# Spectral kernel on one core: the mixed signal stored by groups of eight positions, result tiles taken from two or three groups, wider mode matmuls

## The chip, the core and the metric

One Trainium2 chip, one of its cores. A time is the device time of one execution in microseconds (us). The kernel before: 379.84 us, the median of three runs (379.36 to 381.79). Engines: PE multiplies matrices (its weight loads are listed as PEld), VectorE is DVE, ScalarE is ACT, GpSimd is POOL; SP only issues DMAs here, and POOL issues some.

## The reference

Two layers on x of 8 batches, S = 5696 positions, D = 128 channels. The first convolves every channel with a filter h of the same length; the second mixes 64 Fourier modes, adds the result to its input, and adds a ReLU of a channel product:

```python
L = 2 * S
y = irfft(rfft(x, n=L, axis=1) * rfft(h, n=L, axis=0)[None], n=L, axis=1)[:, :S]
X = rfft(y, axis=1)[:, :64]
Yr = einsum('bmd,mde->bme', X.real, w_r) - einsum('bmd,mde->bme', X.imag, w_i)
Yi = einsum('bmd,mde->bme', X.real, w_i) + einsum('bmd,mde->bme', X.imag, w_r)
u = y + irfft(Yr + 1j * Yi, n=S, axis=1)      # 64 modes, the others zero
out = u + maximum(u @ w_ch, 0)                # float32, 8 x 5696 x 128
```

## The kernel before

A position s is written s = 64 q + p, with q from 0 to 88 and p from 0 to 63. The convolution is done as a transform over q and one over p, with 90 frequencies k. Batches go in four **pairs** `g_` of two (`b` = 0, 1).

*Up to about 255 us*, pair after pair: the transform of x (`a_tile`), the second transform (`second`), the product with the filter (`products`), and the way back over p. The result Z goes to DRAM (`zscr`), and the 64 modes of each pair are summed beside it in one PSUM bank. At the end of a pair two copies with a factor, `XT`, take these modes to SBUF (lines 757 to 760): one of 256 columns on ScalarE, and one of 128 on ScalarE, for the last pair on VectorE. `XT` holds, for each batch, 64 columns of the negated imaginary part, then the real, then the imaginary part.

*The mix* (`mix`, line 828) is 128 matmuls, two for each mode, whose weights are the mode's matrix and whose moving operand are 16 columns of `XT` (two parts of eight batches, gathered from a step of 192 columns). Between its parts PE makes the Z part of the first three u tiles (`u_z` with `alone`). Then the copies Y, eight transposes, and the copies C.

*The last stage* makes u and the result. A **u tile** (`u_tile`, line 809) is one batch, eight values of p and all 89 values of q: 16 matmuls with 89 columns on Z (`ZT`, `S4a`, `S4b`) and two with 356 columns for the modes (`IBs`, `C`), in two of the eight PSUM banks. One copy takes its 712 columns to `UT`, a row of 5696 positions per batch, in natural order: position 64 q + p in column 64 q + p, so that runs of eight columns are written. The copies go to ScalarE and VectorE five to three, and in the last pair to ScalarE alone. A **chunk** of 16 values of p (two u tiles for each batch) is loaded from `zscr` by two DMAs; there are five buffers (`NC`), and chunk i + 5 is asked for once chunk i is used up (`load_zt`).

A **result tile** (`o_tile`, line 863) is four matmuls with 256 columns: the weights are 128 positions of `UT`, 44 columns apart, and the moving operand `WI` holds `w_ch` beside a unit matrix. ScalarE takes the ReLU of one half to `R`, VectorE adds `R` to the other half into an output buffer `O` (seven of 1024 columns for two tiles, four smaller `Os`). One DMA on SP writes two tiles. Since the positions of a tile lie all over the row, it reads all eight groups of u of its batch. A batch has eleven such tiles, and the last 64 positions of the two batches of a pair make a twelfth, short one.

The order is written out by hand (from line 907). A list `todo` holds the result tiles that may be made. In pairs 0 to 2 the loop takes chunk after chunk, in it one batch and then the other; behind each u tile come one or two tiles from the list (`1 + half`), and a pair's tiles are put on the list when the pair is done. So pair 0 has no result tiles. In the last pair one batch is made whole, then the other; each u tile is followed by two tiles, then two or three, and the tiles of batch 0 are listed halfway. What is left at the end follows behind the last u tile.

Both kinds of tiles take their PSUM banks in turn from one ring of four slots (`LSLOT`), two banks each. Every engine executes its instructions in the order recorded; the class `Recorder` puts in the waits from what each instruction reads and writes, an output DMA on SP waits for its additions, and what stands behind it on SP waits too. DMAs of a kind take their semaphores from a ring (`"o"`: 12 for output), and one waits for the one a whole ring before it.

All matmuls have line 323, copies 311 to 317, DMAs 320, ReLUs 893 and additions 894.

Of the kernel before, what the change touches and what calls it, by code (L numbers as in the profile page):

```python
# [4 lines left out]
P = 128  # L5
# [118 lines left out]
def bass_long_conv_fft__then__afno_spectral_mix_kernel(nc, x, h, moe_w_r, moe_w_i, moe_w_ch, out):  # L124
    B, S, D = x.shape
# [167 lines left out]
        return bass.AP(ps, p0 * 4096 + bank * 512 + off, [[4096, n]] + [list(d) for d in dims])  # L293

    R = Recorder(nc)
    for name, n in (("c", 16), ("x", 26), ("z", 10), ("w", 16), ("t", 20), ("s", 8), ("o", 12), ("p", 16), ("q", 10)):
        R.ring(name, n)

    def bank(i):
# [445 lines left out]
    for g_ in range(NP):  # L745
        if g_ == NP - 1:
            load_w(0)
            load_w(1)
        for t in range(NT + LM):
            tick(g_, t)  # L750
            if g_ == 0 and t < 2:
                keep(8, 4)
            assert g_ + 1 < NP or not wp
            if g_ == NP - 1 and t in early:
                pace[:] = [("u", min(t, NT - 1) % NU)]
                early[t]()
        evac(bass.AP(xt, 2 * g_ * XTW + M, [[B * XTW, P], [XTW, 2], [1, P]]), pv(MB, 0, [[P, 2], [1, P]]),
             [bank(MB)], [("xt", g_)], 1.0 / 64, eng="scalar", after=[("ag", k) for k in range(NS + 2 * XN, NK)])
        evac(bass.AP(xt, 2 * g_ * XTW, [[B * XTW, P], [XTW, 2], [1, M]]), pv(MB, M, [[P, 2], [1, M]]),
             [bank(MB)], [("xtn", g_)], -1.0 / 64, eng="vector" if g_ + 1 == NP else "scalar", after=[("ag", k) for k in range(NS + 2 * XN, NK)])  # L760
        if g_ + 1 < NP:
            for j in range(6, 32):
                a_tile(j, [(4, 6, 0, 2)[(j - 7) % 4] if j > 6 else 0], "both" if j == 31 else (A, V)[(j - 6) % 9 % 2])
                if j == 31:
                    second(g_ + 1, 0, 0, DA)
                if wp and j % 2 == 1:
                    dst, src_, ring, tok = wp.pop(0)
                    dma("gpsimd", dst, src_, ring, (), [tok], after=[("as", j)])
# [6 lines left out]
        clear_zt(i)  # L775

    LSLOT = [0, 2, 4, 6]
    NCH = J // ZB
    n_ev = [0]
    ahead = {}  # L780
# [28 lines left out]
    def u_tile(i, b, half):  # L809
        g_, c_ = divmod(i, NCH)  # L810
        t = ahead.get((i, b, half))
        if t is None:
            t = u_z(i, b, half)
        else:
            for hb in range(2):
                u_c(i, b, half, t, hb, False)
        ub = (g_ % 2) * 2 + b
        old = {0: WT, 1: WT, 2: U_ALL, 3: U_ALL}[ub]
        n_ev[0] += 1
        e = "scalar" if n_ev[0] % 8 in (0, 2, 3, 5, 7) or g_ == NP - 1 else "vector"  # L820
        src = pv(t, 0, [[1, NQ], [512, 2], [NQ, 4]])
        evac(bass.AP(u_sb[ub], c_ * ZB + half * 8, [[S, P], [J, NQ], [4, 2], [1, 4]]),
             src, [bank(t), bank(t + 1)], [("u_", ub, 2 * c_ + half)], eng=e, after=once(("u", ub), old))

    XTT = [(n, g_) for g_ in range(NP) for n in ("xt", "xtn")]
    reflect("vector", s4_sb[0], P, 0, ("s4", 0), M_ALL[1:4])
    reflect("scalar", s4_sb[1], PB + RB, 1, ("s4", 1), AST)
    def mix(m0, m1):
        for m in range(m0, m1):
            for ri, first_col in ((0, M + m), (1, m)):  # L830
                mm(pv(6 + m // 32, m % 32 * 2 * B, [[1, 2 * B]]), w_sb[:, (ri * M + m) * D:(ri * M + m + 1) * D],
                   bass.AP(xt, first_col, [[B * XTW, P], [M, 2], [XTW, B]]), ri == 0, ri == 1, WT + XTT, [bank(6 + m // 32)])

    u_z(0, 0, 0, True)
    for n in range(2):
# [19 lines left out]

    n_o = [0]
    o_cur = [0]
    o8_old = [H_ALL] * 2 + [U_ALL] + [G_ALL + ZX] * 2 + [WT] * 2
    o_old = [H_ALL] * 2 + [M_ALL[5:6], U_ALL + [("f1",)]]
    NW = S // P  # L860
    TAIL = S - NW * P

    def o_tile(g_, b, r4):
        ub = (g_ % 2) * 2 + b
        bb = 2 * g_ + b
        t = turns("l", LSLOT)
        i = n_o[0]
        n_o[0] += 1
        full = r4 < NW // 4
        ubs = [ub] if full else [ub, ub + 1]  # L870
        last_ = (g_, b) == (NP - 1, 1)
        wide = r4 < (8 if last_ else NW // 4 // 2 * 2)
        big = wide or (last_ and full)
        h_ = r4 % 2 if wide else 0
        if big:
            if not h_:
                o_cur[0] = turns("o8", list(range(NO8)))
            ob, key, old = o8_sb[o_cur[0]], ("o8", o_cur[0]), o8_old[o_cur[0]]
        else:
            k_ = turns("os", list(range(NO)))  # L880
            ob, key, old = o_sb[k_], ("os", k_), o_old[k_]
        OW = 1024 if big else 512
        n, rows = (4, P) if full else (2, TAIL)
        rd = [("u_", v_, c_) for v_ in ubs for c_ in range(2 * NCH)] + [("wch",), ("i16",)]
        for j in range(n):
            lh = bass.AP(u_sb[ub], 4 * r4 + j, [[S, P], [NW, P]]) if full else u_sb[ubs[j]][:, NW * P:S]
            mm(pv(t + j // 2, (j % 2) * 256, [[1, 256]], 0, rows), lh, WI, True, True, rd, [bank(t + j // 2)])
        bk = [bank(t), bank(t + 1)] if full else [bank(t)]
        rs = r_sb[i % NR]
        rv = bass.AP(rs, 0, [[512, rows], [P, n], [1, P]])  # L890
        ov = bass.AP(ob, h_ * 512, [[OW, rows], [P, n], [1, P]])
        src_r, src_u = pv(t, 0, [[256, n], [1, P]], 0, rows), pv(t, P, [[256, n], [1, P]], 0, rows)
        R.add("scalar", lambda e: e.activation(rv, src_r, RELU), bk, [("r", i % NR)], after=once(("r", i % NR), G_ALL + XTT + [("y", 0), ("y", 1), ("id",)]))  # L893
        R.add("vector", lambda e: e.tensor_tensor(ov, src_u, rv, ADD), bk + [("r", i % NR)],  # L894
              [key + (h_,)], after=once(key, old))
        if wide and not h_:
            return
        w_ = (2 if wide else 1) * 4 * D
        if full:
            dst = bass.AP(out.tensor, out.offset + bb * S * D + (4 * r4 - 4 * h_) * D, [[NW * D, P], [1, w_]])  # L900
            src = ob[:, 0:w_]
        else:
            dst = bass.AP(out.tensor, out.offset + bb * S * D + NW * P * D, [[D, TAIL], [S * D, 2], [1, D]])
            src = bass.AP(ob, 0, [[OW, TAIL], [D, 2], [1, D]])
        dma("sync", dst, src, "o", [key + (v_,) for v_ in range(h_ + 1)])

    todo = []
    NB = NCH * NP
    NW4 = NW // 4
    for g_ in range(NP):  # L910
        last = g_ == NP - 1
        order = [(c_, b) for b in range(2) for c_ in range(NCH)] if last else [(c_, b) for c_ in range(NCH) for b in range(2)]
        for n, (c_, b) in enumerate(order):
            i = NCH * g_ + c_
            for half in range(2):
                u_tile(i, b, half)
                for _ in range((2, 2 + half)[n >= NCH] if last else 1 + half):
                    if todo:
                        o_tile(*todo.pop(0))
            if b == 1 and i + NC < NB:  # L920
                load_zt(i + NC)
            if last and n == NCH - 1:
                todo += [(g_, 0, r4) for r4 in range(NW4)]
        todo += [(g_, 0, NW4)] * last
        todo += [(g_, b, r4) for b in range(1 if last else 0, 2) for r4 in range(NW4)]
        todo += [(g_, 0, NW4)] * (not last)
    while todo:
        o_tile(*todo.pop(0))
    R.add("sync", lambda e: e.nop(), [], [("o8", i, v_) for i in range(NO8) for v_ in range(2)] + [("os", i, 0) for i in range(NO)])
# [31 lines left out]
```

## Time and profile before

| | |
|---|---|
| median of three runs | 379.84 us |
| profiled execution | 378.84 us |
| its span | 377.0 us |
| busy: PE, PEld, DVE, ACT, POOL | 359.5, 279.1, 294.8, 314.1, 75.0 us |
| granted PE clock, mean of the span | 0.99 |
| mix begins; first mode matmul (`IBs`) | 256.58; 263.49 us |
| last u matmul; last addition | 364.20; 373.0 us |

Each row of the profile's groups is a line, an engine, an operation and a shape, with its count, busy time and mean duration; idle time before it is put down to whoever ended it. A time line gives start and duration of each instruction. A busy PE is not a PE at its peak: a matmul's record runs until its last column has left, so records overlap, and what a matmul costs is read from the spacing of starts.

### The profile page before, as it was taken

How to read it: one execution, taken by the hardware profiler on the slowest of the kernel's cores; microseconds unless marked ns; L12 is line 12 of the kernel's file. 1: busy time of each engine (PE TensorE's matmuls, PEld its weight loads, DVE VectorE, ACT ScalarE, POOL GpSimd, SP SyncE). 2: the span in 40 equal slices, each digit the busy share in tenths (PEclk: the TensorE clock that was granted, in tenths of full speed). 3: DMA queues.
4: the chain of work that ended last, by engine and by line, in shares of the span. 5: the costliest groups of instructions: out<-in, count | busy, mean ns of one | idle time of the engine just before them, and what ended most of it. 6: DMA issues, size and time to landing. Idle time of an engine off the chain costs nothing.

```text
span 377.0 us, 12488 instructions
## 1 busy us (share of the span) xinstructions
PE 359.5 (95%) x5370; PEld 279.1 (74%) x5370; DVE 294.8 (78%) x336; ACT 314.1 (83%) x495; POOL 75.0 (20%) x117
## 2 busy tenths in 40 slices
PE   7889899999999999999999999999999999999994
PEld 7878766666866666866667766668899889988873
DVE  3649889988998999989998988873437767756666
ACT  8469789998989997999997999995457776788885
POOL 8713011200743220842311301133000000000000
PEclk9999999999999999999999999998899999999999
DMA  7999979979899997999994999999999999999878
GB/s 146 207 285 369 250 163 238 234 201 269 92 148 206 249 246 206 109 137 218 260 269 136 115 345 359 372 358 384 375 394 351 355 416 407 422 408 379 327 292 330
DMA packets 87048, 103.94 MB, mean 276 GB/s; under 512 B 22730, under 2 KB 72522, under 8 KB 83438
## 3 DMA queue, kind: packets, MB, share of 16 engines
q1 hardware_dynamic: 64610, 81.33, 61.4%
q0 software_dynamic: 22384, 21.83, 35.3%
q8 instruction: 42, 0.69, 0.8%
q14 instruction: 12, 0.10, 0.1%
HBM read 70.61 MB, written 51.12 MB: 323 GB/s over the span
## 4 chain that ended last, share of the span: by engine, by line
PE 72%; ACT 10%; DMA 6%; DVE 5%; POOL 3%; issue 3%; DVEq 0%; POOLq 0%
PE ps L323 72%; ACT As L313 7%; DMA Xr<-in_x_dram 4%; DVE As L317 2%; DMA Xt<-in_x_dram 2%; POOL Xr L320 2%; DVE U L622 1%; ACT Zs L311 1%; ACT Xs L311 1%; POOL Hin L320 1%; DVE Xin L365 1%; DVE Hs L315 1%; ACT R L893 1%; ACT Zt L311 1%; DVE U L655 0%
## 5 line engine op out<-in xcount | busy, mean ns | idle before, releaser
L655 DVE TENSOR_TENSOR U<-Xs,Hs 128x2048 f16<-128x2048 f16 (+1 forms) x73 | 86.6, 1192 | 13.9 <-ACT Xs L311 13.0
L323 PE MATMUL ps<-U,Wc 128*128 128x512 f16 (+1 forms) x368 | 94.1, 376 | 1.4 <-DVE U L622 1.4
L311 ACT CAST Xs<-ps 128x1024 f16<-128x1024 f32 (+1 forms) x77 | 74.8, 979 | 10.0 <-PE ps L323 6.9
L311 ACT CAST Zs<-ps 128x512 f16<-128x512 f32 (+1 forms) x132 | 69.2, 594 | 1.7 <-PE ps L323 1.7
L894 DVE TENSOR_TENSOR O<-ps,R 128x512 f32<-128x512 f32 x81 | 52.3, 684 | 20.1 <-ACT R L893 11.2
L317 DVE TENSOR_SCALAR As<-ps 128x720 f16<-128x720 f32 (+1 forms) x67 | 55.6, 880 | 5.7 <-PE ps L323 4.0
L893 ACT ACTIVATE R<-ps 128x512 f32<-128x512 f32 (+1 forms) x92 | 50.5, 591 | 8.5 <-PE ps L323 8.4
L323 PE MATMUL ps<-F,Xin 128*128 128x180 f16 x512 | 52.4, 250 | 3.8 <-DVE Xin L365 2.4
L323 PE MATMUL ps<-As,M 64*128 64x128 f16 (+2 forms) x1488 | 51.9, 215 | 1.2 <-ACT As L313 1.2
L323 PEld LDWEIGHTS ps<-F,Xin 128*128 128x128 f16 x512 | 44.5, 155 | 11.2 <-DVE As L317 3.0
L313 ACT ACTIVATE As<-ps 128x720 f16<-128x720 f32 (+1 forms) x65 | 45.8, 768 | 7.2 <-PE ps L323 6.7
L323 PE MATMUL ps<-WI,UT 128*128 128x256 f16 x360 | 51.0, 278 | 0.5 <-ACT UT L311 0.4
L323 PEld LDWEIGHTS ps<-U,Wc 128*128 128x128 f16 x368 | 28.7, 97 | 30.3 <-ACT Zs L311 3.7
L311 ACT CAST UT<-ps 128x712 f16<-128x712 f32 x46 | 34.5, 752 | 19.5 <-PE ps L323 18.6
L323 PEld LDWEIGHTS ps<-As,M 64*128 64x128 f16 x1488 | 41.6, 94 | 7.5 <-ACT As L313 1.7
L323 PEld LDWEIGHTS ps<-WI,UT 128*128 128x128 f16 x360 | 39.0, 152 | 3.4 <-issue 1.8
L323 PE MATMUL ps<-IBs,C 128*128 128x356 f16 x128 | 40.5, 326 | 0.1
L320 POOL DMA_DIRECT2D Xt<-in_x_dram x40 | 21.5, 541 | 79.1 <-PE ps L323 78.6
L323 PEld LDWEIGHTS ps<-G,Zs 128*128 128x128 f16 x512 | 26.1, 96 | 14.5 <-ACT Zs L311 2.0
L655 DVE TENSOR_TENSOR U<-ps,Hs 128x2048 f16<-128x2048 f32 x15 | 34.2, 2283 | 0.0
L323 PE MATMUL ps<-G,Zs 128*128 128x128 f16 (+2 forms) x512 | 32.3, 192 | 0.1
L311 ACT CAST Zt<-ps 128x512 f16<-128x512 f32 x52 | 28.5, 624 | 0.3 <-PE ps L323 0.3
(74 smaller groups left out, 487.3 us busy)
## 6 DMA issues: line engine op xcount, KB each, us to landing
out_dram<-O SPq DMA_DIRECT2D x39, 512.0 KB, 7.4
zscr<-Zs SPq DMA_DIRECT2D x62, 256.0 KB, 6.3
zscr<-Zt SPq DMA_DIRECT2D x26, 256.0 KB, 6.0
Xt<-in_x_dram POOLq DMA_DIRECT2D x20, 320.0 KB, 6.8
W<-wscr SPq DMA_DIRECT2D x4, 1024.0 KB, 6.7
ZT0a<-zscr SPq DMA_DIRECT2D x4, 1024.0 KB, 7.8
M<-cM POOLq DMA_DIRECT2D x5, 720.0 KB, 17.4
ZT1a<-zscr SPq DMA_DIRECT2D x3, 1024.0 KB, 8.5
```

The costliest lines, as they stand in the source:

```text
L311: R.add(e, lambda h_: h_.copy(dst, src), reads, writes, after=after)
L313: R.add(e, lambda h_: h_.activation(dst, src, COPY, scale=scale), reads, writes, after=after)
L315: R.add(e, lambda h_: h_.tensor_copy(dst, src), reads, writes, after=after)
L317: R.add(e, lambda h_: h_.tensor_scalar_mul(dst, src, scale), reads, writes, after=after)
L320: R.add(eng, lambda h_: h_.dma_start(dst, src), reads, writes, ring=ring, after=after)
L323: R.add("tensor", lambda h_: h_.matmul(o, l, r, start=st, stop=sp), reads, writes)
L365: R.add("vector", lambda e: e.tensor_copy(bass.AP(x_sb, i * XN * XS, [[XW, NQ], [XS, XN], [1, D]]), src), list(toks) + XZ, [("xin", i)])
L622: R.add("vector", lambda e: e.tensor_tensor(bass.AP(u_s[0], b * 512 + d0, [[2048, P], [1024, 2], [D, n], [1, d1 - d0]]), bass.AP(s_[0], s_ ...
L655: R.add("vector", lambda e: e.tensor_tensor(uv, src, hv, MULT), bk + [("h", t, 0), ("h", t, 1, 0), ("h", t, 1, J)], [("u", i)])
L893: R.add("scalar", lambda e: e.activation(rv, src_r, RELU), bk, [("r", i % NR)], after=once(("r", i % NR), G_ALL + XTT + [("y", 0), ("y", 1 ...
L894: R.add("vector", lambda e: e.tensor_tensor(ov, src_u, rv, ADD), bk + [("r", i % NR)], [key + (h_,)], after=once(key, old))
```

## The change

Three things are changed, and one with them.

1. **`UT` is laid out by groups.** For the first 80 values of q, a u tile (group A of eight values of p, A from 0 to 7) lies in eight rows, one for each p, of 640 columns; in a row group A has columns 80 A to 80 A + 79, one for each q. The last nine values of q keep their natural order behind it. A u tile is now copied by two instructions, one of 640 elements and one of 72. The last pair's copies go to both engines, five to three, as the others'.
2. **Result tiles follow their groups.** Tile (`"m"`, i, h) takes columns 128 i to 128 i + 127 of four of the eight rows, next to each other, so it reads the two or three groups that these columns lie in. It is listed when the last of these groups has been made, from the first pair on; a tile of the last nine q's (`"r"`), and the short one (`"t"`), when all eight are. Behind a u tile come two tiles while more than `BACK` = 2 are listed, and else one. An output buffer is written by one DMA for each group in it, two or three; the ring `"o"` has 24 semaphores.
3. **Modes in rows.** `XT` holds, for each mode, three rows of eight batches side by side, so the two copies that fill it work in runs of two elements, and the mix reads 16 neighbours.
4. In the mix each matmul streams these 16 columns four times (`MC`), into the places of its own mode and of the three behind it, which are then written over by their own matmuls.

```diff
-        evac(bass.AP(xt, 2 * g_ * XTW + M, [[B * XTW, P], [XTW, 2], [1, P]]), pv(MB, 0, [[P, 2], [1, P]]),
+        evac(bass.AP(xt, 2 * g_ + B, [[B * XTW, P], [B, 2], [3 * B, M], [1, 2]]), pv(MB, 0, [[M, 2], [1, M], [P, 2]]),
...
+    QM = 80
+    MR = 8 * QM
...
-        e = "scalar" if n_ev[0] % 8 in (0, 2, 3, 5, 7) or g_ == NP - 1 else "vector"
-        src = pv(t, 0, [[1, NQ], [512, 2], [NQ, 4]])
-        evac(bass.AP(u_sb[ub], c_ * ZB + half * 8, [[S, P], [J, NQ], [4, 2], [1, 4]]),
-             src, [bank(t), bank(t + 1)], [("u_", ub, 2 * c_ + half)], eng=e, after=once(("u", ub), old))
+        e = "scalar" if n_ev[0] % 8 in (0, 2, 3, 5, 7) else "vector"
+        A_ = 2 * c_ + half
+        bk = [bank(t), bank(t + 1)]
+        evac(bass.AP(u_sb[ub], A_ * QM, [[S, P], [4 * MR, 2], [MR, 4], [1, QM]]), pv(t, 0, [[512, 2], [NQ, 4], [1, QM]]),
+             bk, [("u_", ub, A_)], eng=e, after=once(("u", ub), old))
+        evac(bass.AP(u_sb[ub], 8 * MR + 8 * A_, [[S, P], [J, NQ - QM], [4, 2], [1, 4]]),
+             pv(t, QM, [[1, NQ - QM], [512, 2], [NQ, 4]]), bk, [("ur", ub, A_)], eng=e)
...
+    MC = 4
...
-            for ri, first_col in ((0, M + m), (1, m)):
-                mm(pv(6 + m // 32, m % 32 * 2 * B, [[1, 2 * B]]), w_sb[:, (ri * M + m) * D:(ri * M + m + 1) * D],
-                   bass.AP(xt, first_col, [[B * XTW, P], [M, 2], [XTW, B]]), ri == 0, ri == 1, WT + XTT, [bank(6 + m // 32)])
+            for ri, first_col in ((0, (3 * m + 1) * B), (1, 3 * m * B)):
+                n = min(MC, 32 - m % 32)
+                mm(pv(6 + m // 32, m % 32 * 2 * B, [[1, 2 * B * n]]), w_sb[:, (ri * M + m) * D:(ri * M + m + 1) * D],
+                   bass.AP(xt, first_col, [[B * XTW, P], [0, n], [1, 2 * B]]), ri == 0, ri == 1, WT + XTT, [bank(6 + m // 32)])
...
+    BACK = 2
...
+    def groups(i):
+        return range(P * i // QM, (P * i + P - 1) // QM + 1)
...
+            if big:
+                lh = bass.AP(u_sb[ub], (4 * h_ + j) * MR + P * i, [[S, P], [1, P]])
...
+            for A_ in groups(i):
+                f0, f1 = max(P * i, QM * A_), min(P * i + P, QM * A_ + QM)
+                dma("sync", bass.AP(out.tensor, out.offset + (bb * S + J * (f0 - QM * A_) + 8 * A_ + p_at) * D, [[J * D, f1 - f0], [1, w_]]),
+                    ob[f0 - P * i:f1 - P * i, 0:w_], "o", done)
...
                 u_tile(i, b, half)
-                for _ in range((2, 2 + half)[n >= NCH] if last else 1 + half):
+                for _ in range(2 if len(todo) > BACK else 1):
                     if todo:
                         o_tile(*todo.pop(0))
+                A_ = 2 * c_ + half
+                for m in range(NM):
+                    if groups(m)[-1] == A_:
+                        todo += [(g_, b, "m", m, h_) for h_ in range(2)]
+                if A_ == 7:
+                    todo.append((g_, b, "r", 0, 0))
+                    if b == 1:
+                        todo.append((g_, 0, "t", 0, 0))
```

## The prediction

> **What bounds the kernel now.** The profiled execution took 378.84 us: a span of 377.0 and 1.84 around it. All sums are made against 378.84; the median of the three runs, 379.84, is 1.0 higher. About 1% (3.8 us) is what a measurement of this kernel can tell from no change.
>
> Everything that the change touches lies after 255 us, so I cut the span there into stages (busy time by stretch): rest of the half-clock phase, rest of pair 0, pair 1, pair 2, pair 3, and what follows the last u matmul.
>
> ```profile
> core 0: us, PE busy (x) PEld busy (x) DVE busy (x) ACT busy (x) POOL busy (x), PEclk, DMA share, GB/s
> 263.49:267.14 3.65, 3.65 (x28) 2.47 (x26) 1.73 (x3) 1.41 (x2) 0.00 (x0) 0.50 1.02 357
> 267.14:278.89 11.75, 11.75 (x218) 10.42 (x216) 4.50 (x5) 5.26 (x7) 0.00 (x0) 1.00 0.98 385
> 278.89:304.92 26.03, 26.03 (x380) 23.63 (x377) 18.31 (x27) 19.02 (x32) 0.00 (x0) 1.00 0.96 367
> 304.92:331.38 26.46, 26.46 (x382) 23.79 (x379) 19.32 (x29) 19.30 (x34) 0.00 (x0) 1.00 1.02 414
> 331.38:364.20 32.82, 32.74 (x424) 28.25 (x422) 21.36 (x35) 28.40 (x51) 0.00 (x0) 1.00 0.88 355
> 364.20:373.60 9.40, 7.30 (x54) 5.33 (x51) 8.26 (x14) 7.91 (x14) 0.00 (x0) 1.00 0.86 340
> ```
>
> PE fills every stage but the last. The first row shows a granted clock of 0.50. The chain of waits, in order of time, says the same and shows the end:
>
> ```profile
> 263.09 90.94 PE ps L323 x1292
> 354.03 0.08 issue
> 354.11 10.27 PE ps L323 x130
> ...
> 364.40 0.76 ACT UT L311
> 365.16 0.04 issue
> 365.21 2.45 PE ps L323 x18
> ...
> 370.23 2.40 ACT R L893 x4
> 372.63 0.04 DVEq L115
> 372.67 0.33 DVE O L894
> ```
>
> So: PE until 364.20, then 8.8 us in which ScalarE and VectorE work off 13 result tiles, then 4.0 us from the last addition (373.0) to the span's end, for the last output DMAs. For the prices I read the order of instructions around the end:
>
> ```profile
> 333.00 0.75 ACT L311 CAST UT<-ps 128x712 f16<-128x712 f32 x1 [0.40 <-PE ps L323]
> 333.65 1.09 ACT L893 ACTIVATE R<-ps 128x512 f32<-128x512 f32 x2
> ...
> 366.93 6.67 DVE L894 TENSOR_TENSOR O<-ps,R 128x512 f32<-128x512 f32 x11 [0.17 <-issue]
> ```
>
> An instruction starts before the one ahead has drained. Spacings: ScalarE 0.65 us for a u copy of 712 elements (333.00 to 333.65), 0.49 for a ReLU of 512 (three in 1.58, two in 1.09); VectorE 0.60 for an addition (eleven in 6.67), 0.81 for a u copy (one at 325.36, the next instruction at 326.17). On PE a u tile takes 0.98 (first mode matmuls of neighbouring steps at 280.35, next step's result matmuls at 281.33), a result tile of four matmuls 0.435 (eight in 0.87), and 0.035 goes at each turn from one to the other. PE's work before 364.20 is then: pair 0: 13 x 0.983 + 3 x 0.31 (three u tiles have their Z part done ahead) = 13.7, plus 1.8 for the half clock; pairs 1 to 3: 48 x 1.018 = 48.9; 76 full tiles x 0.435 and three short ones x 0.22 = 33.7. Together 98.1 of the 100.7 us. The missing 2.6 are waits, nearly all in pair 3 (16.3 + 14.1 = 30.4 worked, 32.7 spent: 0.14 a step); pairs 1 and 2 wait 0.1 and 0.4 in all, about 0.02 a step.
>
> **The change part by part.**
>
> *Wide mode matmuls.* The mix streams 16 columns in each of 128 matmuls:
>
> ```profile
> 259.16 2.05 PE L323 MATMUL ps<-XT,W 128*128 128x16 f16 x64
> ```
>
> They follow each other every 0.0295 us. At 60 or more columns the rows give 0.43 to 0.47 ns a column (89 columns every 0.0415, 356 every 0.152), so 64 columns are about 0.030: +0.1 us, bounds 0 and 128 x 0.012 = 1.5. What it may do is to the clock, which was 0.50 from 260.32 to 267.14 and 1.00 for 250 us before. In the 3.41 us before the drop (half of its length) PE was never idle for over 0.2 us, yet streamed only 16 x 89 + 92 x 16 = 2,900 columns, 35% of the 8,200 that 2.4 a ns allow; in the 3.41 us before that, some 44%, and no drop followed. With 64 columns the share in that stretch is 16 x 89 + 92 x 64 = 7,300, 89%, and in the next (rest of the mix, Z matmuls, transposes, first mode matmuls) some 60%. I take it that the clock stays. It gives 1.8 us on 263.49 to 267.14, and 0.4 on the eight transposes (0.105 apart at half clock, 0.053 at full) that the C copy waits for. The Trainium skill ("TensorE: Matmul & The Clock Gate", Part 1) has the clock fall after an idle window of 3.4 us; by idleness alone it would not have fallen here and the wide matmuls would gain nothing. The trace differs: it shows the fall under a busy PE, and the measurement decides. The half clock lasted twice 3.41 us, which agrees with the page's window. The same page's Part 4 (PE-mode transpose) says that transposes do not count as busy in the same way; no row here shows that.
>
> *XT copies in pairs.* As many elements (ScalarE 0.386 for 256, VectorE 0.290 for 128, both on the path to the mix), in runs of two. Bounds 0 and +0.3; +0.1, near 0, since the As copies in short runs cost 0.785 for 720, the rate of UT. First mode matmul: 263.49 - 0.4 + 0.2 = 263.3.
>
> *u copied in two parts.* 640 and 72 elements for 712. On the spacings above (0.0008 us an element on ScalarE, 0.00103 on VectorE): 0.59 + 0.14 and 0.74 + 0.15, so +0.08 each, 64 times. Bounds: 0, and +0.21 if the short one costs the full 0.27 of an XT copy of 128. ScalarE then holds 40 x 0.73 + 92 x 0.49 = 74 us and VectorE 24 x 0.89 + 92 x 0.60 = 77 of some 105: PE hides both, unless a tile waits for just that copy.
>
> *Tiles begin early.* PE's work is the same, 92 tiles, 64 u tiles; unit-stride weights bring nothing, since the 0.109 a matmul of 256 columns is already their rate. What moves: tiles run from the first pair, and behind the last u matmul stand five full and one short instead of twelve and one. So the end behind it is 0.2 (PE to ScalarE) + 0.73 + 0.59 (first ReLU) + 0.05 + 5 x 0.60 + 0.41 = 5.0 instead of 8.8; and seven full tiles, 7 x 0.435 = 3.0, come ahead of it. PE before the last u matmul: 61 x 1.018 + 3 x 0.31 + 83 x 0.435 + 3 x 0.22 = 99.8.
>
> *New waits.* A tile now reads groups copied a step or two earlier. On VectorE such a copy is queued behind up to three additions (1.8 us), and behind the waiting tile's matmuls stand the next u tile and, through it, the next copies. In steps with one tile, PSUM slots also come round sooner: a step lasts 1.45 us, a slot is reused two steps later, and a tile's matmuls, ReLU and addition need 0.44 + 0.2 + 0.6 + 0.1 + 0.7 = 2.0 without any queue. Bounds a step: 0.02 (pairs 1, 2, with the same 1.44 tiles a step, but old groups) and 0.14 (pair 3, where ScalarE was as full as PE). I take 0.07: the load is that of pairs 1 and 2, the tightness more that of pair 3. 64 x 0.07 = 4.5 (1.3 to 9.0), where 2.6 were.
>
> *Output DMAs.* 53 become some 107, of 16 to 128 rows. An issue holds SP for 0.33 us when nothing is backed up; 107 x 0.33 and the loads are some 45 of 110 us. The Z loads stand behind them on SP, but have four chunks (22 us) of lead, against 8 to 11 us to landing.
>
> ```profile
> out_dram<-O SPq DMA_DIRECT2D x20, 512.0 KB, 9.3
> ZT3a<-zscr SPq DMA_DIRECT2D x1, 1024.0 KB, 10.7
> ```
>
> This is the stretch 283 to 331, moving 390 GB/s. Seven output buffers refilled every 2.4 us give 16.7 us for production and landing, so the cover is a few us. Four more pieces behind the last additions: +0.3. The weights of the result tiles, which the first one now needs near 265, landed at 262.2 (issued on POOL at 255.1): 2.5 us of cover; later, it would wait for them.
>
> **Sum.** Last u matmul at 263.3 + 99.8 + 4.5 = 367.6 (was 364.2): +3.4; tail -3.8; DMA end +0.3. That is -0.1; I say **378.9**, within 1%.
>
> **Rivals.**
> *PE alone* (faster). The waits are as in pairs 1 and 2 (-3.2: 375.7) or nothing (-4.5: 374.4); 374.8. For it: ScalarE and VectorE have a quarter of their time to spare. Against: a fresh group has to pass a queue. 0.24.
> *Fresh groups stall PE* (slower). At 0.14 a step throughout, +4.5: 383.4. Its place is the result matmul that waits for the last of its groups; it decides once a copy on VectorE or ScalarE ends later than the next u tile's 1.0 us. If the short copy costs 0.27, this is the likelier. 0.14.
> *The clock falls all the same.* +2.2: 381.1. For it: 60% of columns in the second stretch rests on transposes. 0.13.
> *Output pieces slow the DMAs.* From pair 0 to 2 demand is some 430 to 460 GB/s (one chunk of 1.48 MB in 5.5 to 6.9 us, one tile of 0.26 in 1.2 to 1.45), over the 390 moved; the backlog, about 3 MB at its peak, fits. At 338 GB/s (the lowest slice of this stage) it would reach 5.5 MB, 16 us, and the output buffers would hold PE by some 5 us: 383.9. The Trainium skill ("DMA: Bandwidth & Descriptors", Bandwidth) asks for 1 MiB a transfer and gives 32% of the peak for 64 KB, which is the size of the smallest piece here; no row of before shows a stream of such pieces. Against: pieces of 256 KB landed in 2.8 to 3.0 us at the end. 0.08.
> *The forecast*: 0.41. That the tiles don't move early is excluded: the instruction order has them.
>
> Faster by over 1% (under 375.0): 0.20, most of the first rival and the low edge of mine; slower by over 1% (over 382.6): 0.20, the second and fourth with some of the third; within: 0.60. Range 374.5 to 383.9.
>
> **What would show it.** Granted clock 1.00 from 255 to 373; UT copies in two forms, 128x640 near 0.69 and 128x72 near 0.22 us; the last u copy near 367.8, not 364.4, and about 5 us from it to the last addition; PE waiting for UT or O in nearly every step, some 4 to 5 us in all; landings of 8 to 13 us. Wrong if PE waits under 2 us or over 8, if the clock drops, or if DVE waits for output landings.

## The result and the profile after

The changed kernel takes **394.21 us** (median of six, 392.0 to 397.77), the kernel before 379.90 beside it (six, 379.02 to 381.79): a ratio of **1.038** (95% interval 1.035 to 1.041), slower by 14 us, where 378.9 and at most 383.9 were forecast. The profiled execution took 395.94 us: a span of 394.1 and 1.84 around it.

The mix does not begin at the same time in each execution (256.58 and 258.20 us in these two profiles), so stages are compared from there. "First mode matmul" is the first `IBs` matmul, "last u copy" the start of the last copy of a u tile (of its 640 elements in the changed kernel), "last addition" its end.

| us | before | after |
|---|---|---|
| mix begins | 256.58 | 258.20 |
| first mode matmul | 263.49 | 264.66 |
| last u copy begins | 364.40 | 379.88 |
| last addition ends | 373.59 | 384.69 |
| span | 377.0 | 394.1 |
| first mode matmul to last u copy | 100.9 | 115.2 |
| last u copy to last addition | 9.2 | 4.8 |
| last addition to the end of the span | 3.4 | 9.4 |

The tail became shorter by 4.4 us, as the change lets one expect. But the stretch that PE should fill became 14.3 us longer, and the end 6.0. The busy times by stretch of the changed kernel show where (the first three stretches are roughly pairs 0, 1 and 2, the next two pair 3, and the last is what follows PE's last matmul):

```profile
core 0: us, PE busy (x) PEld busy (x) DVE busy (x) ACT busy (x) POOL busy (x), PEclk, DMA share, GB/s
270.00:293.00 23.00, 22.79 (x328) 18.72 (x324) 16.19 (x29) 16.94 (x38) 0.00 (x0) 1.00 0.97 348
293.00:317.00 24.00, 22.57 (x325) 18.58 (x324) 16.63 (x30) 16.84 (x37) 0.00 (x0) 1.00 0.96 333
317.00:345.00 28.00, 24.50 (x350) 20.60 (x347) 17.42 (x33) 17.82 (x39) 0.00 (x0) 1.00 0.99 350
345.00:365.00 20.00, 16.07 (x188) 12.62 (x186) 11.47 (x21) 10.43 (x23) 0.00 (x0) 0.83 0.99 356
365.00:383.00 18.00, 17.29 (x231) 13.80 (x229) 12.71 (x23) 14.10 (x31) 0.00 (x0) 1.00 0.87 266
383.00:394.00 11.00, 0.10 (x1) 0.00 (x0) 1.69 (x4) 0.67 (x2) 0.00 (x0) 0.63 0.79 248
```

PE is no longer full: between 270 and 365 it is busy 85.9 of 95 us. The column that explains it is the last one. The DMA share stands at 0.96 to 0.99, as in pairs 0 to 2 before (0.96 to 1.02), yet what is moved is 333 to 356 GB/s, where the kernel before moved 367 to 414. So a busy share near one says here only that the DMA engines have work, not how much they move. The waits of 255 to 394 name the path from there to PE (total, times, longest):

```profile
engine line waited for: us in total, times, longest us
ACT R L911 <- PE ps L323: 24.7, 24, 5.8
...
PEld ps L323 <- issue: 11.8, 22, 3.9
DVE O L912 <- DMA out_dram<-O: 9.9, 4, 3.6
PE ps L323 <- DVE O L912: 9.1, 8, 3.7
```

VectorE waits for an output buffer whose DMAs have not landed (four times, 9.9 us); PE then waits for VectorE to give its PSUM banks back (9.1). The kernel before had no wait of VectorE on an output DMA. The chain of waits shows one such round:

```profile
305.61 0.70 DVE O L912
306.32 0.24 SPq L320
...
306.60 8.32 DMA out_dram<-O
...
315.12 0.70 DVE O L912
315.82 0.14 issue
315.95 4.89 PE ps L323 x70
```

The same returns at 321.97 (9.21 us) and at 340.42 (8.69). During the last of these waits the granted clock falls to 0.50, from 348.2 to 355.0: the 0.83 of the fourth stretch. At the end SP still has pieces to issue when the work is done: the last addition ends at 384.7, the last issue from a wide buffer starts at 390.0, and SP issues until 391.6. All issues from the wide buffers, with the landings:

```profile
L320 SPq DMA_DIRECT2D out_dram<-O x98: 314/626/2359, 269.9 to 390.0; - x98
...
DMA to landing us min/median/max: 2.8/7.3/9.5
```

An issue (minimum, median and maximum in ns) holds SP for 626 ns in the median, where before it was 333:

```profile
L320 SPq DMA_DIRECT2D out_dram<-O x42: 332/333/872, 283.6 to 373.6; - x42
```

### The profile page after: what moved, and what is told of

The parts are those of the page before. It is cut to its first block, busy times and chain, and to the rows that moved or that the text cites. A ratio compares the mean times of both kernels' runs of the same rounds, so it can differ in the third digit from the quotient of the medians.

```text
span 394.1 us, 12637 instructions
## 1 busy us (share of the span) xinstructions
PE 358.9 (91%) x5370; PEld 271.8 (69%) x5370; DVE 301.5 (77%) x366; ACT 313.4 (80%) x529; POOL 75.3 (19%) x117
## 4 chain that ended last, share of the span: by engine, by line
PE 55%; DMA 14%; ACT 13%; DVE 7%; issue 4%; POOL 3%; SPq 1%; DVEq 0%; POOLq 0%; ACTq 0%
PE ps L323 55%; DMA out_dram<-O 7%; ACT As L313 6%; DMA Xr<-in_x_dram 4%; DVE As L317 2%; DMA Xt<-in_x_dram 2%; ACT Zs L311 2%; DMA zscr<-Zs 2%; POOL Xr L320 2%; ACT Xs L311 2%; DVE O L912 1%; ACT Zt L311 1%; DVE U L622 1%; ACT UT L311 1%; SPq L320 1%
## 5 line engine op out<-in xcount | busy, mean ns | idle before, releaser
L912 DVE TENSOR_TENSOR O<-ps,R 128x512 f32<-128x512 f32 x80 | 53.1, 686 | 36.6 <-ACT R L911 17.1
L911 ACT ACTIVATE R<-ps 128x512 f32<-128x512 f32 (+1 forms) x92 | 51.8, 598 | 24.7 <-PE ps L323 24.7
L311 ACT CAST UT<-ps 128x640 f16<-128x640 f32 x80 | 32.4, 459 | 14.2 <-PE ps L323 13.8
L323 PEld LDWEIGHTS ps<-WI,UT 128*128 128x128 f16 x360 | 31.3, 100 | 10.7 <-issue 5.3
```

What stands on the lines that cost most here:

```text
L311: R.add(e, lambda h_: h_.copy(dst, src), reads, writes, after=after)
L323: R.add("tensor", lambda h_: h_.matmul(o, l, r, start=st, stop=sp), reads, writes)
```

## The experiments

Three things could have caused it: SP, which issues 132 DMAs after 266 us instead of 75; the way in which the pieces lie in DRAM or on the partitions; or the early tiles themselves. "Rate" is what the DMAs moved in the stretch from 283 to 345 us; the changed kernel's is 345 GB/s, that of the kernel before 391.

**1. Half of the pieces on another queue.** Every second output buffer's pieces are issued from POOL.

```diff
-dma("sync", ..., "o", done)
+dma(("sync", "gpsimd")[o_cur[0] % 2], ..., ("o", "x")[o_cur[0] % 2], done)
```

> The kernel after, with the output DMAs of every second wide buffer issued by POOL instead of SP; same pieces, same addresses, same order of work. Three theories for the 14 us. Issue: in the profile of after SP spends 113 of the 126 us from 266 to 392 us issuing 132 DMAs (0.86 us each), the last output DMA goes out 6.6 us behind the last addition, and VectorE waits for output buffers; with half of the pieces on POOL, SP issues some 80 and the time falls to 379 to 384. Pitch: the rows of a piece lie 32 KB apart in DRAM and the writes themselves are slow (4 KB packets took 0.215 us on the mean from 366 to 390 us, 0.160 in the kernel before); then the issuer doesn't matter: 392 to 396. Few partitions: a piece of 16 to 80 partitions is drawn from too few of them at once; the issuer doesn't matter either: 390 to 396.

Measured: 392.61 us (392.08 to 393.14), ratio 1.032 (1.027 to 1.037). The rate rose to 384 GB/s, and VectorE still waited for output DMAs (4.3 us in two waits). With SP relieved of a third of its DMAs, 1.6 us come back, no more than the scatter of the changed kernel's own runs. The last addition comes 2.9 us earlier after the mix (123.6 us for 126.5), but the end is hardly shorter (9.1 us for 9.4; in its last 3.5 no DMA moves anything). So relieving SP in part does not bring the 14 back; experiments 3 and 4 test SP without a second queue.

**2. One DMA for each output buffer.** The tiles, their order and everything else stay; a buffer's 128 rows go out in one DMA, to rows 22 KB apart as before the change (so the output's rows are not in the reference's order). With it, the same pieces as in the changed kernel but to rows 22 KB apart, and one DMA to rows 32 KB apart, the changed kernel's distance.

```diff
-for A_ in groups(i):
-    f0, f1 = ...
-    dma("sync", bass.AP(..., [[J * D, f1 - f0], [1, w_]]), ob[f0 - P * i:f1 - P * i, 0:w_], "o", done)
+dma("sync", bass.AP(out.tensor, out.offset + bb_at, [[44 * D, P], [1, w_]]), ob[:, 0:w_], "o", done)
```

> The kernel after, with one output DMA of 128 rows for each buffer, written to the places that the kernel before used (rows 22 KB apart); the computed values are the same, but most rows of the output stand in another place than the reference's. Takes away number, pitch and few partitions at once. All three theories: 377 to 382, which is the sum of the prediction without the output DMAs; if it stays over 386, the loss is in the order of the tiles (fresh groups that PE waits for), not in the output.

> The kernel after, with the same two or three pieces for each buffer, but their rows 22 KB apart in DRAM as in the kernel before, so rows of the output stand in other places than the reference's. Issue: unchanged, 392 to 396. Pitch: 377 to 383. Few partitions: unchanged, 392 to 396.

> The kernel after, with one output DMA of 128 rows for each buffer, rows 32 KB apart in DRAM as in after; rows of the output stand in other places than the reference's. Issue: 377 to 382, as with rows 22 KB apart. Pitch: 390 to 396. Few partitions: 377 to 382.

Measured: one DMA, 22 KB: **379.81 us** (379.29 to 381.43), ratio 1.000 (0.997 to 1.003). Pieces, 22 KB: 395.31, ratio 1.039 (1.033 to 1.045). One DMA, 32 KB: 380.09 (378.99 to 381.54), ratio 1.000 (0.997 to 1.003). So the whole loss is in the cutting of the output DMAs, and the distance of the rows in DRAM has no part in it that these runs can tell. Busy times by stretch of the kernel with one DMA, 22 KB:

```profile
core 0: us, PE busy (x) PEld busy (x) DVE busy (x) ACT busy (x) POOL busy (x), PEclk, DMA share, GB/s
270.00:293.00 23.00, 22.76 (x319) 18.41 (x318) 16.47 (x29) 17.12 (x37) 0.00 (x0) 1.00 1.01 395
293.00:317.00 24.00, 23.48 (x338) 19.24 (x335) 17.11 (x32) 17.13 (x37) 0.00 (x0) 1.00 1.02 413
317.00:345.00 28.00, 27.69 (x391) 22.45 (x389) 20.28 (x38) 20.18 (x44) 0.00 (x0) 1.00 1.02 407
345.00:365.00 20.00, 19.77 (x271) 15.68 (x270) 14.57 (x26) 15.12 (x34) 0.00 (x0) 1.00 0.88 354
```

PE is busy 93.7 of the same 95 us, the rate is back at 395 to 413 GB/s, and no engine waits for an output DMA.

**3. As many DMAs, but tiny ones.** The kernel with one DMA, and for each piece that the changed kernel has more, one DMA of 16 rows of 512 bytes (8 KB) to a scratch tensor.

```diff
+for k in range(len(groups(i)) - 1):
+    n_x[0] += 1
+    dma("sync", bass.AP(scr, n_x[0] * 16 * P, [[P, 16], [1, P]]), ob[0:16, 0:P], "o", done)
```

> As the run with one output DMA for each buffer (379.8), with one or two small DMAs more behind each: 16 partitions, 8 KB in all, to an unused place in DRAM. So SP issues as many output DMAs as in after (57 more), nearly the same bytes. If the number of DMAs is what costs (SP's issue, or a fixed price for each on its queue): 392 to 396. If it is that the data itself is drawn from few partitions: 380 to 383.

Measured: 381.27 us (380.38 to 383.17), ratio 1.003 (1.000 to 1.006), rate 408 GB/s. As many issues as in the changed kernel cost some 1.5 us, a tenth of the loss, at the edge of what four runs can tell from nothing.

**4. Two DMAs a buffer: halves, or every second partition.** Both have 64 rows of 4 KB, 256 KB in each DMA, and write the same rows as the kernel with one.

```diff
+for p0 in (0, 64):   # halves
+    dma(..., [[44 * D, 64], [1, w_]] from row p0, ob[p0:p0 + 64, 0:w_])
+for p0 in (0, 1):    # even and odd
+    dma(..., [[88 * D, 64], [1, w_]] from row p0, bass.AP(ob, p0 * OW, [[2 * OW, 64], [1, w_]]))
```

> One buffer written by two DMAs of 64 rows: partitions 0 to 63, then 64 to 127, rows 22 KB apart (rows of the output stand in other places than the reference's). 41 more DMAs than with one for each buffer. Number: 386 to 392. Few partitions (the 16 DMA engines draw a transfer from half of the partitions at a time): 386 to 394.

> The same two DMAs of 64 rows for each buffer, but the first takes the even partitions and the second the odd ones, so each spans all 128 (rows of the output stand in other places than the reference's). Number: the same as with halves, 386 to 392. Few partitions: 380 to 382, since each DMA engine then draws from its own partitions as with 128 rows.

Measured: halves **388.01 us** (387.95 to 388.08), ratio 1.021 (1.018 to 1.024); even and odd **380.78** (380.26 to 382.23), ratio 1.003 (1.001 to 1.005). Number and size of the DMAs are equal, so neither is the cause of the 7.2 us between them. The DMAs of 283 to 345, halves first (in the second line the count of output DMAs, the size, and the median from issue to landing):

```profile
DMA packets 5697, 23.27 MB, mean 375 GB/s; under 512 B 963, under 2 KB 1219, under 8 KB 4285
...
out_dram<-O SPq DMA_DIRECT2D x38, 256.0 KB, 9.1
```

and even and odd:

```profile
DMA packets 6127, 25.33 MB, mean 409 GB/s; under 512 B 1040, under 2 KB 1296, under 8 KB 4565
...
out_dram<-O SPq DMA_DIRECT2D x46, 256.0 KB, 11.8
```

The slower kernel moves 375 GB/s against 409, though its DMAs land sooner (9.1 us in the median, against 11.8). The time from issue to landing does not show the loss; the rate does.

**5. Partitions or DRAM?** The two kernels of 4 differ in DRAM as well: a half writes a stretch of 1.4 MB, every second partition one of 2.8 MB. The next two cross this: halves of the partitions to the rows that even and odd wrote, and the other way round.

```diff
-[[44 * D, 64], [1, w_]] from row p0,          ob[p0:p0 + 64, 0:w_]
+[[88 * D, 64], [1, w_]] from row p0 // 64,    ob[p0:p0 + 64, 0:w_]
-[[88 * D, 64], [1, w_]] from row p0,          bass.AP(ob, p0 * OW, [[2 * OW, 64], [1, w_]])
+[[44 * D, 64], [1, w_]] from row 64 * p0,     bass.AP(ob, p0 * OW, [[2 * OW, 64], [1, w_]])
```

> Two DMAs for each output buffer, partitions 0 to 63 and 64 to 127 as in the kernel with halves (388.01), but to rows 44 KB apart, which are the places in DRAM that the kernel with even and odd partitions (380.78) writes (the output lies in other rows than the reference's). If the part of the partitions is the cause: 387 to 389, the DMAs moving some 375 GB/s in 283 to 345. If the stretch of DRAM is: 380.3 to 381.5 at some 409 GB/s.

> Two DMAs for each output buffer, from even and from odd partitions as in the kernel with 380.78, but to 64 rows 22 KB apart, which are the places in DRAM that the kernel with halves (388.01) writes (the output lies in other rows than the reference's). If the part of the partitions is the cause: 380.3 to 381.5 at some 409 GB/s in 283 to 345. If the stretch of DRAM is: 387 to 389 at some 375 GB/s.

Measured: halves to far rows 389.06 us (388.91 to 390.13), ratio 1.027 (1.023 to 1.030), 377 GB/s; even and odd to near rows 381.42 (380.31 to 383.65), ratio 1.005 (1.002 to 1.008), 408 GB/s. The partitions decide: at equal rows they make 6.6 and 8.3 us. The place in DRAM makes 1.1 us at most.

**6. Which partitions?** Either any run of neighbours is slow, or only one that stays on one side of partition 64. Three DMAs a buffer, of 64, 32 and 32 rows: the large one across partition 64, on one side of it, or (as a control) all three spread. And two DMAs of 64 rows, both from partitions 32 to 95.

```diff
+((32, 64), (0, 32), (96, 32))     # first partition, rows: middle and ends
+((0, 64), (64, 32), (96, 32))     # half and quarters
+((0, 2, 64), (1, 4, 32), (3, 4, 32))   # first partition, step, rows: even and fourths
+ob[32:96, 0:w_] in both DMAs of the halves   # middle twice
```

> Three DMAs for each output buffer, to the rows of the kernel with one whole DMA: partitions 32 to 95, 0 to 31 and 96 to 127 (the output lies in other rows than the reference's). Kernels so far: whole 379.81, halves 388.01, even and odd 380.78. If any run of neighbours is slow: 388 to 392, with output waits on VectorE, DMAs moving 345 to 375 GB/s in 283 to 345. If only a run that stays on one side of partition 64 is slow: half of the bytes are freed of it, so some 380.8 + half of the 7.2 between halves and even and odd, and 0.5 for the third DMA: 383 to 386, and 385 to 400 GB/s. The Trainium skill ('SBUF — State Buffer', Door 1: The DMA port swizzle) lets partitions 0 to 63 and 64 to 127 each reach 8 of 16 ports, and 32 to 95 all 16; that is the second case.

> Three DMAs for each output buffer as in the kernel with 32 to 95 apart, of the same sizes, but partitions 0 to 63, 64 to 95 and 96 to 127 (the output lies in other rows than the reference's). By both theories as the halves or some worse: 388 to 392, 345 to 380 GB/s in 283 to 345. What tells the theories apart is the difference to the kernel with 32 to 95: none if any run of neighbours is slow, 3 to 6 us if only one that stays on a side of partition 64.

> Three DMAs for each output buffer of 64, 32 and 32 rows, as in the kernels with 393.81 and 395.43, but from spread partitions: every second, and twice every fourth (the output lies in other rows than the reference's). If neighbours are the cause: 381 to 383 at some 405 GB/s in 283 to 345. If three DMAs of so few rows are slow whatever the partitions: 388 to 394 at some 355 GB/s.

> Two DMAs of 64 rows for each output buffer as in the kernel with halves (388.01), but both from partitions 32 to 95 (what the other partitions hold is not written, and the rows lie in other places than the reference's). If any run of neighbours is slow: 387 to 390 at some 375 GB/s in 283 to 345. If only a run on one side of partition 64 is: 380.3 to 382 at some 408 GB/s.

Measured: middle and ends 393.81 us (392.0 to 394.6), ratio 1.035 (1.032 to 1.039), 354 GB/s; half and quarters 395.43 (395.18 to 396.65), ratio 1.041 (1.039 to 1.044), 354 GB/s; even and fourths 384.07 (383.69 to 387.54), ratio 1.012 (1.008 to 1.017), 407 GB/s; middle twice **381.65** (380.9 to 382.49), ratio 1.005 (1.003 to 1.007). The DMAs of 283 to 345 in the last one:

```profile
DMA packets 6069, 25.11 MB, mean 405 GB/s; under 512 B 1025, under 2 KB 1281, under 8 KB 4517
...
out_dram<-O SPq DMA_DIRECT2D x46, 256.0 KB, 11.2
```

64 neighbours across partition 64 are as good as even and odd (405 GB/s beside 409); 64 neighbours on one side are not (375). So it is the side that counts for 64 rows. That agrees with the Trainium skill ("SBUF — State Buffer", Door 1: The DMA port swizzle), by which partitions 0 to 63 reach the even and 64 to 127 the odd ones of 16 ports, eight each, while 32 to 95 or every second partition reach all. But the terms do not add up. Of the three DMAs with neighbours, moving the large one across partition 64 won back only 1.6 of 11.4 us, against my 3 to 6, and left the rate at 354 GB/s: the two runs of 32 on one side cost 9.7 (393.81 to 384.07), more than both halves did (388.01 to 380.78, 7.2). Why the shorter runs are dearer stays open; 32 neighbours across partition 64 were not tried.

The number of DMAs has a price too: three spread ones cost 4.3 us over one (384.07 to 379.81), where two cost 1.0. The profiles show where. In us, each from one profile:

| | mix to last addition | last addition to the end |
|---|---|---|
| one DMA | 116.8 | 3.8 |
| even and odd | 116.5 | 5.0 |
| even and fourths | 116.5 | 7.3 |
| middle twice | 117.2 | 5.0 |
| halves | 121.3 | 7.9 |
| middle and ends | 124.6 | 10.6 |
| half and quarters | 125.3 | 10.7 |
| the changed kernel | 126.5 | 9.4 |

Two or three spread DMAs do not delay the last addition. They cost behind it, where SP issues the last pieces one by one and no work covers it. SP's last issues with one DMA, and with even and fourths:

```profile
373.79 1.08 SPq L320 DMA_DIRECT2D out_dram<-Os  x2
...
369.54 9.09 SPq L320 DMA_DIRECT2D out_dram<-O  x13
378.68 1.27 SPq L320 DMA_DIRECT2D out_dram<-Os  x2
```

They end 0.8 us behind the last addition in the first (374.08) and 5.5 in the second (374.49). The one-sided runs cost in both columns.

**7. Early tiles with output DMAs over all partitions.** The first 64 values of q in place of 80 are laid out so that a tile is exactly the two groups of a chunk, columns 2 q + half. One DMA then writes a buffer's 128 rows to their own places; a second kernel uses two, from even and odd partitions. 25 values of q are left for the late tiles, so each batch has three of them.

```diff
-QM = 80
+QM = 64
-evac(bass.AP(u_sb[ub], A_ * QM, [[S, P], [4 * MR, 2], [MR, 4], [1, QM]]), ...
+evac(bass.AP(u_sb[ub], c_ * 8 * P + half, [[S, P], [4 * P, 2], [P, 4], [2, QM]]), ...
-lh = bass.AP(u_sb[ub], (4 * h_ + j) * MR + P * i, [[S, P], [1, P]])
+lh = bass.AP(u_sb[ub], 8 * P * i + (4 * h_ + j) * P, [[S, P], [1, P]])
+dma("sync", bass.AP(out.tensor, out.offset + at_ * D, [[J * D, QM], [8 * D, 2], [1, w_]]), ob[:, 0:w_], "o", done)
-                todo.append((g_, b, "r", 0, 0))
+                todo += [(g_, b, "r", r_, 0) for r_ in range(NR4)]
```

> Groups of 64 values of q in place of 80, so that a result tile of 128 positions is exactly the two groups of one chunk (columns 2 q + half), begins once both are made, and one output DMA writes the 128 rows of a buffer to their own places; the other 25 values of q give three tiles and the short one for each batch, behind all eight groups, as before. So this has the early tiles, the new layout and the wide mix of the changed kernel and writes the same positions of the output, but no DMA draws on a part of the partitions. Theory (pieces from a part of the partitions are the cause, early tiles in themselves gain nothing): 379 to 381, no DMA wait on VectorE, SP busy near 35 us. Rival (the fine-grained order of the tiles and its effect on loads is what costs, whatever the output DMAs are): 390 or more. Second rival (three tiles of the rest, which the last chunk frees all at once, lengthen the tail by 2 tiles): 381 to 382.

> As the kernel with one DMA for each buffer of a chunk's two groups, but two DMAs, one for each group; they draw on the even and on the odd partitions. If the number of DMAs and their 64 rows matter little so long as they reach over all partitions: 0.5 to 1.5 us more than with one DMA, 380 to 382. If pieces that go to their own places in the output are slow whatever partitions they draw on: 386 or more, with DMA waits on VectorE.

Measured: one DMA 382.37 us (382.1 to 383.63), ratio 1.009 (1.006 to 1.012), 403 GB/s; two DMAs 382.67 (382.56 to 382.78), ratio 1.009 (1.007 to 1.011), 405 GB/s. Neither has a wait on an output DMA: 12 of the 14 us are gone with the output in its place. Both are still above the kernel before. Against the kernel with one DMA and groups of 80, this one has 0.8 us more behind the last u copy (5.7 for 4.9, the second rival's mechanism) and 1.6 more ahead of it; what makes the 1.6 was not taken apart.

**8. The clock, alone and taken away.** The kernel before with `XT` in rows and the wide mix, nothing else; and the kernel with one DMA, with `MC` = 1 instead of 4.

```diff
+ the edits of XT (two copies) and of the mix, as in the change     # before with wide mix
-MC = 4
+MC = 1                                                             # one DMA, narrow mix
```

> The kernel before with the third part of the change alone: modes in rows, 64 columns in each matmul of the mix. The prediction's term: the clock stays at 1.00 through 260 to 267 us, -2.0 us, 377.9 beside 379.9. If the clock falls all the same: 0 to +0.6.

> The kernel with early tiles and one DMA of 128 rows for each output buffer (379.81; its output lies in other rows than the reference's), but every matmul of the mix streams 16 columns once instead of four times; the modes stay in rows. Theory (the wide matmuls keep the clock and give 1.8 us, the early tiles take that much): clock at 0.50 from about 260 to 267, 381.4 to 382.0. Rival (the rows of neighbours in XT or something else of the change keeps the clock, or the clock does not matter where tiles begin early, since the first steps wait anyway): 379.5 to 380.3.

Measured: before with wide mix **378.45 us** (377.44 to 378.79; before 379.79), ratio 0.995 (0.994 to 0.997), the fastest of all. One DMA, narrow mix: 379.86 (378.95 to 382.23), ratio 1.001 (0.998 to 1.003), the same as with the wide mix, which is what the rival said and not the theory. The clock did fall there, around the same place, but for one step of 3.41 us instead of two:

```profile
core 0: us, PE busy (x) PEld busy (x) DVE busy (x) ACT busy (x) POOL busy (x), PEclk, DMA share, GB/s
258.00:260.30 2.30, 2.30 (x87) 2.30 (x84) 0.76 (x1) 1.80 (x2) 0.02 (x1) 1.00 1.07 361
260.30:263.50 3.20, 2.98 (x59) 2.81 (x56) 1.12 (x3) 0.60 (x1) 0.00 (x0) 0.58 1.09 386
263.50:267.20 3.70, 3.22 (x34) 2.20 (x33) 2.15 (x4) 2.04 (x5) 0.00 (x0) 0.90 1.00 355
```

From the mix to the last addition the narrow one took 117.1 us and the wide one 116.8. So the rows of neighbours in `XT` do not keep the clock, the streamed columns do. What the clock is worth came out at 1.4 us in the kernel before and at 0.3, not clear of noise, here. Whether that is because the half clock lasted one step and not two, or because the first tiles wait here anyway, was not separated.

**9. Late tiles in the new layout.** The kernel with one DMA, its tiles listed and interleaved as before the change: PE's order is that of the kernel before with the wide mix, and only the layout of u with its two copies a tile is left.

```diff
-for _ in range(2 if len(todo) > BACK else 1):
+for _ in range((2, 2 + half)[n >= NCH] if last else 1 + half):
+# a pair's tiles are listed when the pair is done; last pair: batch 0 halfway, copies on ScalarE
```

> The kernel with one DMA of 128 rows for each output buffer (its output lies in other rows than the reference's), but with the result tiles listed and interleaved as in the kernel before: a pair's tiles when the pair is done, in the last pair one batch halfway, copies of the last pair on ScalarE alone. PE's order is then that of the kernel before with the wide mix (378.45); what is left of the change is the layout of u by groups and its two copies for each tile. From the mix's first matmul to the last addition that kernel took 115.6 us, the one with early tiles and whole DMAs 116.8. Theory (fresh groups make the waits of early tiles, the second copy of 72 elements is hidden beside PE): 115.6 to 116.0 from mix to last addition, 378.2 to 379.0 in all. Rival (the 64 extra copies, 0.14 to 0.15 us each on engines that are full in the last pair, cost by themselves): 116.8 to 118, 379.6 to 381.

Measured: 379.35 us (378.86 to 381.43), ratio 1.000 (0.998 to 1.002). From the mix to the last addition, us, with its parts:

| | to first mode matmul | to last u copy | to last addition | sum |
|---|---|---|---|---|
| before | 6.9 | 100.9 | 9.2 | 117.0 |
| before with wide mix | 6.5 | 99.9 | 9.2 | 115.6 |
| new layout, late tiles, one DMA | 6.5 | 100.4 | 9.2 | 116.1 |
| new layout, early tiles, one DMA | 6.5 | 105.4 | 4.9 | 116.8 |
| the changed kernel | 6.5 | 115.2 | 4.8 | 126.5 |

116.1 lies between the two expectations: the second copy seems not quite hidden (0.5 us), and the early tiles seem to take another 0.7. Both are differences of one profile each, and kernels with early tiles that differ only in whole or spread output DMAs lie up to 0.5 apart in this sum (116.5 to 117.0), so neither is sure. What is plain is that the early tiles gain nothing even with whole output DMAs: the tail is 4.3 us shorter and the stretch before it 5.0 longer.

## Why the prediction was wrong

It failed in one step, **Output DMAs**, which put some 54 more DMAs (57 in fact) at 0.33 us of SP each, hidden, and 0.3 us at the end, with the DMAs moving as much as before. They cost 14.4 us (394.21 to 379.81). The prediction's own sign for that came: VectorE waited for output landings, 9.9 us. Point by point:

*Output DMAs.* I asked for the time of an issue and for the demand in GB/s, and took for the supply the 390 GB/s that the stretch 283 to 331 of the kernel before had moved, with nearly all of its output in DMAs over 128 partitions. That rate does not hold for the new pieces: with them it was 345. The issue price was wrong as well (626 ns in the median for 333), but that is not the loss: in the even and odd kernel, only 1.0 us slower than one DMA, it is 597, and relieving SP brought 1.6 us at most. Of each batch's 640 rows of early tiles, the twelve pieces put 320 into runs that stay on one side of partition 64 (48, 32, 16, 64, 64, 16, 32 and 48 rows); the other four pieces, of 80 rows, lie across it. The runs show that such one-sided runs lower the rate and that more DMAs alone cost 1.0 us (two a buffer) to 4.3 (three); here there are 2.4. The split between the two is not measured for just these pieces, but the table in 6 allows an estimate from the profiles (which lie 16.2 us apart, where the medians are 14.4). Up to the last addition, spread DMAs cost nothing, so the 9.7 us there (126.5 for 116.8) are put down to the one-sided runs and what they set off. Against that stands only the kernel with tiny extras, with 118.5 us in the slowest of its four runs. Behind the last addition the changed kernel takes 5.6 us more, and 1.2 to 3.5 of them are what two or three spread pieces cost.

*The fourth rival*, pieces that slow the DMAs, named the right place. Its supposed rate of 338 GB/s was nearly the measured one, and its mechanism (output buffers hold VectorE, then PE) is what the waits show. It was too small and too unlikely. It priced 5 us where PE was held; that part is 9.8 (115.2 for 105.4), up to 2.5 of it the half clock from 348 to 355, in which PE was busy for 4.9 us. It had nothing for the end, where the rate stays low and SP still issues: 9.4 us from the last addition to the end, 3.8 in the kernel with one DMA (377.9 - 374.08), so 5.6. And where it gave a cause, it was the size of a transfer. By the Trainium skill ("DMA: Bandwidth & Descriptors", Bandwidth) 64 KB would have been the trouble; the trace does not agree, since DMAs of 256 KB went at 375 or at 409 GB/s by their partitions alone, and 8 KB ones beside whole buffers left 408.

*The rest of the sum* can be read from the kernel with one DMA. Time from the first mode matmul to the last u copy: predicted 104.5 (99.8 of work, 4.5 of waits, 0.2 to the copy), measured 105.4, so by difference the waits are 5.4 us or 0.08 a step, inside the bounds of 1.3 to 9.0 and near the 0.07 taken. The tail from the last u copy: predicted 4.8 (5.0 less the 0.2), measured 4.9. The prediction read the end of the last addition before as 373.0; its record begins at 372.9 and ends at 373.59. So the tail before was 9.2 from the last u copy, not 8.6, and the end behind it 3.4, not 4.0; the two errors cancel in the sum. From the mix the last addition came 0.2 us earlier (116.8 for 117.0), where the sum had 0.4 (+3.4 - 3.8). That kernel's 379.81 is within 1 us of the forecast of 378.9, in part by luck: the stretch was 0.9 longer than predicted, and the tail gained 4.3 where 3.8 were put.

*Wide mode matmuls.* The 44% of columns read in the 3.41 us with no drop behind them are some 54% by the trace, which changes nothing in the argument. The clock stayed at 1.00 from 255 us until PE waited at 348, so the third rival fell. The size was off: 2.0 predicted, 1.4 measured alone. The way to the first mode matmul gave 0.4 for the predicted 0.2; the stretch behind it gave 1.0 (100.9 to 99.9) for 1.8, and in pair 2 of that kernel PE sat idle for 0.6 us of the difference.

*Split copies* were put at no cost: 0.5 in one profile. *PE alone* fell: with whole output DMAs the kernel took 379.81 us, not 374.8. *Fresh groups stall PE* fell by its size: 0.08 a step, not 0.14.

## What to carry to other kernels

When a change cuts a DMA into pieces, ask which partitions each piece takes: with runs of 64 rows that stay below or above partition 64 this kernel moved 375 GB/s, with pieces of the same number and size that cross it or are spread 405 to 409. Shorter runs on one side did worse. Price it from the rate of a stage (GB/s at a DMA share near one), not from the time of an issue (626 ns in the slow kernel, 597 in a fast one) or to a landing (earlier in the slow one). Then ask where more DMAs have no work to hide behind: here that was the end, behind the last addition. Test each part of a change alone: here the one small gain, the wide mix (1.4 us), was hidden under a loss ten times its size.

## What the runs showed of the hardware that I had not expected

- Two DMAs of 64 rows of 4 KB for each buffer: 388.0 and 389.1 us from partitions 0 to 63 and 64 to 127, 380.8 and 381.4 from even and odd, 381.7 from 32 to 95. The rows' distance in DRAM (22, 32, 44 KB) changes 1.1 us at most.
- The DMA share was 0.96 to 0.99 at 333 to 356 GB/s and 1.01 to 1.02 at 395 to 413, so it hardly shows the loss. Output packets of 4 KB from 366 to 390 us took 0.215 us in the mean in the changed kernel, and 0.16 before.
- Landings were later (12.6 us in the median) in the fast kernel with one DMA, and earlier (7 to 8) in the slow one.
- More DMAs can be nearly free: 8 KB extras, as many as the change adds, cost 1.5 us, and a second spread DMA for each buffer 1.0. A third then cost 3.3 more; in the profiles it delays only the end (7.3 us behind the last addition, for 5.0).
